# Inverse transform of a spectral mixer: 64-row products in pairs for the odd residues, and folds in two steps

## The chip, the cores and the metric

The kernel runs on one core of a Trainium2 chip. The metric is the device time of one execution in microseconds. The engines are TensorE (PE, with its weight loads as PEld), VectorE (DVE), ScalarE (ACT), GpSimd (POOL) and SyncE (SP); the last issues most transfers. Matmuls write to PSUM, of which the kernel uses eight banks: four called acc, two fa, two fb.

## The reference

Two mixers work on the same shape of input, 2048 rows by 512 columns in bf16, and a gate mixes them row by row:

```
g = sigmoid((x * gate_w).sum(-1, keepdims=True))        # x = A_x
a = irfft2(rfft2(x) * (w_r + 1j * w_i), s=(2048, 512))  # axes: rows, columns; stored as bf16
h = layernorm(B_x)                                      # over the 512 columns
u = gelu(einsum("bsd,sf->bdf", h, w1) + b1)             # s = 2048, f = 1792
b = (einsum("bdf,fs->bds", u, w2) + b2).transpose(0, 2, 1)
out = g * a + (1 - g) * b
```

In this kernel the gate, the filter and the layernorm all read A_x.

## The kernel before

Rows are split as s = 512 q + 4 p + r, with q and r from 0 to 3 and p the partition. A tile of 128 rows is one pair (q, r).

Four lines of work share the engines.

- The token MLP: 224 matmuls of 512 columns for the first layer (L716, into acc, fa and fb), a GELU on ScalarE (L732), and 224 matmuls' worth of 512 columns for the second (L1028), whose results ScalarE evicts with gate and bias (L1034). The last tile is cut into 256, 128 and 128 columns (acc, fa, fb), and VectorE finishes it (L1041).
- The forward transform: radix-4 sums over q on VectorE, matmuls with cosine and sine tables over p (L565 to L568), a second radix-4 step, and the column transform (L664).
- The spectral product with W, all on VectorE (L831 to L853), followed by a radix-4 step of the inverse (L596 to L612).
- The inverse transform, in three stages. The first (lines 885 to 923) multiplies the spectrum, the tile B, with the table ti, for each residue r, each column parity h and two sets of wavenumbers: lt = 0 holds the even ones, lt = 1 the odd ones. Rows p below 64 of lt = 0 carry the wavenumbers 4p, rows from 64 on 2 + 4(p - 64). For even r each product has 128 columns and VectorE folds the results into the tile zz (zf, L931 to L937). For odd r (L903) each product has 256 columns, two accumulate (real and imaginary), and ScalarE casts the bank straight into zz (L918). For lt = 0 and odd r the second 128 table columns repeat the first with the sign turned for rows from 64 on. The second stage (fq, L943 and L944) sums and subtracts over lt and writes the products' sums z. The third (L986 to L990) multiplies z with the table tg; ScalarE evicts with the gate (L994); VectorE then folds each pair of tiles: an edge copy (L1009), two operations into a buffer es (L1010, L1011), two from es back (L1012, L1013), and finally the sum with the MLP's output (L1047). The last pair, called late, also adds the bias (L1007).

The order of the work is decided when the kernel is built. Every piece is a task with an engine, a duration, what it reads and writes, a priority and the buffers it allocates and frees (add, in the class Plan). A list scheduler (Plan.order) walks through time with these durations; on each engine it places the ready task with the lowest priority number whose buffers are free. The tasks are then emitted in that order, and each engine works through its own in it. The second layer's matmuls have high priority numbers (20 and more) and fill whatever PE time the transform (priorities 0 to 4) leaves. The buffers acc, fa, fb, es and the weights wa, wb are counted in caps; NES is the number of es buffers. In the first inverse stage, before the change, a product of lt = 0 takes a bank fa and one of lt = 1 a bank fb.

Of the kernel before, what the change touches and what calls it, by code (L numbers as in the profile page):

```python
# [13 lines left out]
BF16 = mybir.dt.bfloat16  # L14
F32 = mybir.dt.float32

P = 128
# [5 lines left out]
L = 256  # L23
# [7 lines left out]
def ti_at(r):  # L31
    return (0, 1024, 512, 1920)[r], (512, 896)[r % 2]
# [106 lines left out]
class Plan:  # L139
# [11 lines left out]
    def add(self, eng, dur, emit, reads=(), writes=(), prio=0.0, alloc=(), free=(), nbytes=0, after=(), late=0.0):  # L151
        t = Task()
        t.late = late
        t.eng, t.dur, t.emit, t.prio = eng, dur, emit, prio
        t.alloc, t.free, t.nbytes = tuple(alloc), tuple(free), nbytes
        t.users, t.end, t.ready = [], None, 0.0
        deps = set(after)
        for k in reads:
            if k in self.last_w:
                deps.add(self.last_w[k])  # L160
            self.readers.setdefault(k, []).append(t)
        for k in writes:
            if k in self.last_w:
                deps.add(self.last_w[k])
            deps.update(self.readers.get(k, ()))
            self.last_w[k] = t
            self.readers[k] = []
        deps.discard(t)
        t.deps = deps
        self.tasks.append(t)  # L170
        return t
# [73 lines left out]
def tt(n):  # L245
    return 0.07 + n / 1920.0
# [10 lines left out]
def act(n, ptr=0):  # L257
    return 0.065 + 0.09 * ptr + n / 1200.0


def mm(*ns):
    return sum(max(n, 62) / 2400.0 + 0.0025 for n in ns)
# [3 lines left out]
def tiny(k):  # L266
    return 0.09 * k + 0.06
# [3 lines left out]
def kernel(  # L271
# [14 lines left out]
    V, A, T = nc.vector, nc.scalar, nc.tensor  # L286
# [7 lines left out]

    pool = ctx.enter_context(tc.tile_pool(name="sb", bufs=1))
    psum = ctx.enter_context(tc.tile_pool(name="ps", bufs=1, space=bass.MemoryType.PSUM))
    NES = 1

    def sb(shape, dt, tag, bufs=1):
        return pool.tile(shape, dt, tag=tag, name=tag, bufs=bufs)  # L300

    def ps(shape, dt, tag, bufs):
        return psum.tile(shape, dt, tag=tag, name=tag, bufs=bufs)
# [4 lines left out]
    add = pl.add  # L308
    t = {}
# [64 lines left out]
    for r in range(4):  # L374
# [3 lines left out]
        else:  # L378
            for qs in ((0,), (1,), (2, 3)) if r == 1 else ((0, 1, 2, 3),):
                c = slice(qs[0], qs[-1] + 1)  # L380
# [93 lines left out]
    for r in range(4):  # L474
# [3 lines left out]
        for b, qs in enumerate(groups):  # L478
# [8 lines left out]
            for j in js:  # L487
# [14 lines left out]
                if j == 8:  # L502
# [8 lines left out]
                    after=[rect[0, 0]] if j == 4 else ())  # L511
# [23 lines left out]
            for j in js:  # L535
                if j in HACT:
                    add("ACT", 0.71, lambda j=j: A.activation(t["h"][:, j // 4, j % 4, :], t["x"][:, j // 4, j % 4, :], ActF.Identity,  # L537
                                                                  bias=t["nmr"][:, j:j + 1], scale=t["rstd"][:, j:j + 1]),
                        reads=xb + [("rstd", *g)] + mvk, writes=[("h", j)], prio=-0.5 + 0.1 * r)
# [198 lines left out]
    gates = []  # L738
# [136 lines left out]
    for lt in range(2):  # L875
# [5 lines left out]
        if lt == 0:  # L881
            add("SP", 0.5, lambda: dma(t["B"][0:1, 0].rearrange("p e (c v) l -> p (e c) (v l)", c=2), t["s8"][P - 8:P]),
                reads=["s8"], writes=[("T", 0, 0), ("T", 0, 1)], prio=0, nbytes=8192)

    i1t = {}
    for rs, h in ((0, 0), (0, 1), (1, 0), (1, 1)):
        for r in (rs, rs + 2):
            for lt in range(2):
                tag = ("fa", "fb")[lt]

                def i1(h=h, r=r, lt=lt, tag=tag):
                    if "zz" not in t:
                        t["zz"] = sb([P, 2, 2, 2, 2, 2, 2, P], BF16, "X")
                        t["ze"] = sb([P, 2, 2, 2, 2, L], BF16, "h")
                    p1 = t["i1", h, r, lt] = ps([P, 2, L], F32, tag, 2)
                    o, w = ti_at(r)
                    ti = t["ti"][:, o:o + w]
                    for v in range(2):
                        d = lambda c: t["B"][:, lt, r, 2 * c + v, h:L:2]
                        if r % 2:  # L900
                            for c in range(2):
                                f = (2 * c if lt == 0 else 5 - c) * P
                                T.matmul(p1[:, v], lhsT=d(c), rhs=ti[:, f:f + L], start=(c == 0), stop=(c == 1))  # L903
                        else:
                            u = ti[:, 256 * lt:256 * lt + 256]
                            if r == 0 and lt == 0:
                                T.matmul(p1[:, v, 65:256], lhsT=d(1), rhs=t["ti"][:, 2816:3007], start=True, stop=False)
                                T.matmul(p1[:, v, 128:192], lhsT=d(0), rhs=u[:, 66:130], start=False, stop=True)
                                T.matmul(p1[:, v, 0:65], lhsT=d(0), rhs=u[:, 0:65], start=True, stop=True)
                            else:  # L910
                                T.matmul(p1[:, v, P:], lhsT=d(1), rhs=u[:, P:], start=True, stop=True)
                                T.matmul(p1[:, v, 0:P], lhsT=d(0), rhs=u[:, 0:P], start=True, stop=True)
                i1t[h, r, lt] = add("PE", mm(*([256] * 4 if r % 2 else [128] * 4 if r or lt else [191, 64, 65] * 2)), i1, reads=[("T", lt, r % 2), "ti"] + ([("T", lt, 1)] if r == 2 else []), writes=[("i1", h, r, lt)], prio=3, alloc=[tag])

                def i1ev(h=h, r=r, lt=lt):
                    if r % 2:
                        o = t["zz"][:, 1, h, lt, :, :, r // 2, :]
                        A.copy(o, t["i1", h, r, lt][:].rearrange("p v (k a) -> p v k a", k=2))  # L918
                    else:
                        o, i = t["ze"][:, h, r // 2, lt], t["i1", h, r, lt][:]  # L920
                        if r == 0 and lt == 0:
                            o, i = o.rearrange("p v (n w) -> p v n w", w=2), i.rearrange("p v (w n) -> p v n w", w=2)
                        A.copy(o, i)
                add("ACT", act(512), i1ev, reads=[("i1", h, r, lt)] + pbk, writes=[("zz" if r % 2 else "ze", h, r, lt)], prio=1.7, free=[tag], after=[lined])

            if r % 2 == 0:
                def zf(h=h, r=r):
                    e = t["ze"][:, h, r // 2]
                    k0, k1 = (t["zz"][:, 0, h, :, :, k, r // 2, :] for k in range(2))
                    if r == 0:  # L930
                        V.tensor_copy(k0[:, :, :, 0], e[:, :, :, 0])  # L931
                        V.tensor_copy(k1[:, :, :, 0], e[:, :, :, P])
                        V.tensor_add(k0[:, :, :, 1:P], e[:, :, :, 1:P], e[:, :, :, P + 1:L])
                        V.tensor_sub(k1[:, :, :, P - 1:0:-1], e[:, :, :, 1:P], e[:, :, :, P + 1:L])
                    else:
                        V.tensor_add(k0, e[:, :, :, 0:P], e[:, :, :, P:L])
                        V.tensor_sub(k1[:, :, :, ::-1], e[:, :, :, 0:P], e[:, :, :, P:L])  # L937
                add("DVE", 2 * tt(512) + (tiny(2) if r == 0 else 0), zf, reads=[("ze", h, r, lt) for lt in range(2)], writes=[("zz", h, r, lt) for lt in range(2)], prio=3.55)

        def fq(rs=rs, h=h):  # L940
            z = xph(h)[:, 2048 * rs:2048 * rs + 2048].rearrange("p (q v n) -> p q v n", q=4, v=2)
            a, b = (t["zz"][:, rs, h, i].rearrange("p v k r a -> p k v (r a)") for i in range(2))
            V.tensor_add(z[:, 0:4:3], a, b)  # L943
            V.tensor_sub(z[:, 1:3], a[:, ::-1], b[:, ::-1])  # L944
        add("DVE", 2 * tt(1024), fq, reads=[("zz", h, r, lt) for r in (rs, rs + 2) for lt in range(2)] + [("T", 0, 0), ("T", 0, 1), ("T", 1, 0), ("T", 1, 1)],
            writes=[("z", rs, h)] + ([] if rs else ["pp" if h else "xs"]), prio=3.6)
# [27 lines left out]
    for p in range(NJ // 2):  # L974
# [23 lines left out]
        def tb2j(j0=j0):  # L998
            tbuf(j0)
            return t["tb_"][:, j0:j0 + 3:2]  # L1000

        def es(p=p, j0=j0, late=late, tb2j=tb2j):
            e, s = eo_v(p), sb([P, 2, 2, 2, P], BF16, "es", NES)
            o = tb2j() if late else e
            if late:
                for i in range(2):
                    V.tensor_scalar_add(e[:, i, 0, 0:129], e[:, i, 0, 0:129], t["ombb2"][:, j0 + 2 * i:j0 + 2 * i + 1])  # L1007
            o = o.rearrange("p j h (k d) -> p j (h k) d", k=2)
            V.tensor_copy(s[:, :, :, :, 0], e[:, :, :, 0:129:128].rearrange("p j h k -> p j k h"))  # L1009
            V.tensor_add(s[:, :, 0, :, 1:P], e[:, :, :, 1:P], e[:, :, :, P + 1:L])  # L1010
            V.tensor_sub(s[:, :, 1, :, P - 1:0:-1], e[:, :, :, 1:P], e[:, :, :, P + 1:L])  # L1011
            V.tensor_add(o[:, :, 0:4:3], s[:, :, :, 0], s[:, :, :, 1])  # L1012
            V.tensor_sub(o[:, :, 2:0:-1], s[:, :, :, 0], s[:, :, :, 1])  # L1013
        add("DVE", 0.2 + tiny(1) + 4 * tt(512) + (0.3 if late else 0), es, reads=(k1 + ["omg"]) if late else [],
            writes=ko if late else k1, prio=4, alloc=["es"], free=["es"], after=gates if late else ())

        for i, j in enumerate((j0, j1)):
            n = 2 * p + i
# [77 lines left out]
```

## Time and profile before

| | us |
|---|---|
| median of three runs | 126.31 (126.26 to 126.35) |
| the profiled execution | 126.59 |
| its span, first to last instruction | 124.8 |
| TensorE busy | 121.2 (97% of the span) |
| VectorE busy | 113.4 (91%) |
| ScalarE busy | 82.6 (66%) |

The granted TensorE clock was 1.000 over the span. The first inverse stage lies at about 90.4 to 99 us, the third stage and the folds at 99 to 118, and the last store is issued at 122.4. A row of the timeline gives start, length, engine, line, operation and output from input; in a group's row, the count, the busy time, the mean of one in ns and the idle time before it follow. The recorded duration of a matmul includes its way through the array, so neighbouring ones overlap; the distance between two starts is what one costs in a stream. The chain is followed back from the last instruction and says which work set the end.

### The profile page before, as it was taken

What the parts mean: (1) busy time and instruction counts of PE and PEld (TensorE: products, weight loads), DVE (VectorE), ACT (ScalarE), POOL (GpSimd) and SP (SyncE); (2) the same over time, 40 slices, a digit from 0 to 9 for tenths busy, and PEclk for the clock granted to TensorE, in tenths of its full rate; (3) what the DMA queues carried; (4) which work ended last, traced back from release to release, by engine and by line L of the source; (5) the groups of instructions that cost most, each with busy time, mean ns of one, the idle gap of its engine ahead of it and who ended that gap; (6) DMA issues with size and microseconds to landing.
All of it is one profiled execution on the core that took longest, in us unless ns stands there. A gap on an engine that the chain in (4) does not pass through costs nothing.

```text
span 124.8 us, 2188 instructions
## 1 busy us (share of the span) xinstructions
PE 121.2 (97%) x773; PEld 68.8 (55%) x773; DVE 113.4 (91%) x274; ACT 82.6 (66%) x169; POOL 0.2 (0%) x4
## 2 busy tenths in 40 slices
PE   7999999999999999999999999999999999999990
PEld 2345655555655466744455555555578767655590
DVE  1889999999989999999999999999979999999961
ACT  3795889699999999999520003742289999952200
POOL 0000000000000000000000000000000000000000
PEclk9999999999999999999999999999999999999999
DMA  4998999994649936799999900000000000011751
GB/s 122 347 302 277 397 395 389 375 294 86 145 87 302 266 74 156 226 411 414 417 420 415 377 17 0 0 5 0 3 0 0 0 5 0 0 63 45 318 205 47
DMA packets 18202, 23.09 MB, mean 185 GB/s; under 512 B 2174, under 2 KB 15888, under 8 KB 18192
## 3 DMA queue, kind: packets, MB, share of 16 engines
q1 hardware_dynamic: 17616, 22.34, 52.6%
q10 hardware_dynamic: 576, 0.62, 1.6%
q8 instruction: 6, 0.10, 0.3%
q14 instruction: 4, 0.03, 0.1%
HBM read 20.84 MB, written 2.10 MB: 184 GB/s over the span
## 4 chain that ended last, share of the span: by engine, by line
PE 97%; DVE 0%; issue 0%
PE acc L1028 33%; PE acc L716 31%; PE fb L716 6%; PE fb L1028 5%; PE fa L361 4%; PE fa L716 3%; PE fa L664 1%; PE fb L664 1%; PE fa L903 1%; PE fa L566 1%; PE fb L903 1%; PE fa L565 1%; PE fb L990 1%; PE fa L990 1%; PE fa L568 1%; PE fa L567 1%
## 5 line engine op out<-in xcount | busy, mean ns | idle before, releaser
L716 PE MATMUL acc<-h,wb 128*128 128x512 bf16 x112 | 27.0, 379 | 0.0
L1028 PE MATMUL acc<-gl,wb 128*128 128x512 bf16 (+1 forms) x98 | 24.5, 372 | 0.0
L1028 PE MATMUL acc<-gl,wa 128*128 128x512 bf16 (+1 forms) x98 | 23.8, 372 | 0.0
L1034 ACT ACTIVATE x<-acc,ombb,omg 128x512 bf16<-128x512 f32 x12 | 9.1, 782 | 20.8 <-PE acc L1028 20.8
L1028 PEld LDWEIGHTS <-wa 128*128 128x128 bf16 x126 | 13.4, 113 | 9.9
L1028 PEld LDWEIGHTS <-wb 128*128 128x128 bf16 x126 | 13.3, 114 | 9.2
L716 PE MATMUL acc<-h,wa 128*128 128x512 bf16 x64 | 17.4, 385 | 0.0
L716 PEld LDWEIGHTS <-wb 128*128 128x128 bf16 x112 | 10.7, 98 | 10.3
L716 PEld LDWEIGHTS <-wa 128*128 128x128 bf16 x112 | 10.4, 99 | 10.5 <-issue 0.7
L571 ACT CAST xp<-fa 128x512 bf16<-128x512 f32 x16 | 9.1, 584 | 2.4 <-PE fa L568 2.3
L746 ACT ACTIVATE x<-x 128x512 bf16<-128x512 bf16 x16 | 10.0, 649 | 0.0
L716 PE MATMUL fb<-h,wa 128*128 128x512 bf16 x32 | 9.9, 379 | 0.0
L489 DVE BATCH_NORM_STATS2 stats<-x 128x6 f32<-128x512 bf16 x12 | 8.1, 676 | 1.9 <-DMA x<-in_A_x_dram 1.9
L732 ACT ACTIVATE gl<-acc,b1f 128x512 bf16<-128x512 f32 x11 | 7.7, 701 | 2.8 <-PE acc L716 2.8
L537 ACT ACTIVATE h<-x,nmr,rstd 128x512 bf16<-128x512 bf16 x11 | 8.4, 808 | 1.1 <-DVE nmr L528 1.1
L716 PE MATMUL fa<-h,wa 128*128 128x512 bf16 x16 | 6.3, 392 | 0.0
L664 PEld LDWEIGHTS <-X 128*128 128x128 bf16 x64 | 4.7, 98 | 2.2
L994 ACT ACTIVATE B<-fa,g 128x512 bf16<-128x512 f32 x8 | 5.8, 727 | 0.0
L994 ACT ACTIVATE B<-fb,g 128x512 bf16<-128x512 f32 x8 | 5.8, 719 | 0.0
L361 PE MATMUL fa<-const-float32-0.0 128*128 128x512 bf16 x10 | 4.4, 629 | 0.8 <-PEq L1080 0.8
L671 ACT CAST X<-fb 128x512 bf16<-128x512 f32 x8 | 5.1, 638 | 0.0
L671 ACT CAST X<-fa 128x512 bf16<-128x512 f32 x8 | 5.1, 634 | 0.0
(176 smaller groups left out, 235.9 us busy)
## 6 DMA issues: line engine op xcount, KB each, us to landing
wb<-in_B_w_dram SPq DMA_DIRECT2D x11, 512.0 KB
wa<-in_B_w_dram SPq DMA_DIRECT2D x7, 512.0 KB
wa<-in_B_w_dram SPq DMA_DIRECT2D x2, 896.0 KB
wb<-in_B_w_dram SPq DMA_DIRECT2D x4, 384.0 KB
out_dram<-x SPq DMA_DIRECT2D x3, 512.0 KB
x<-in_A_x_dram SPq DMA_DIRECT2D x2, 512.0 KB
wa<-in_B_w_dram SPq DMA_DIRECT2D x4, 224.0 KB
rot<-dft_ti SPq DMA_DIRECT2D x1, 768.0 KB
```

Of the source, the lines that this page charges most:

```text
L361: T.matmul(pw[:], lhsT=zero[:, 0:1].to_broadcast([P, P]), rhs=zero[:, 0:1].to_broadcast([P, D]), start=True, stop=True)
L489: V.bn_stats(out=t["stats"][:, j, :], in_=t["x"][:, j // 4, j % 4, :])
L537: add("ACT", 0.71, lambda j=j: A.activation(t["h"][:, j // 4, j % 4, :], t["x"][:, j // 4, j % 4, :], ActF.Identity, bias=t["nmr"][:, j:j ...
L571: add("ACT", act(512), lambda r=r, dq=dq: A.copy(xe(r)[:, :, :, dq, :], t["pa", r, dq][:]), reads=[("pa", r, dq)], writes=[("X", r, dq)], ...
L664: T.matmul(pb[:, k % 2, k // 2], lhsT=t["X"][:, lt, EX[e], c, k, :], rhs=tbl(k, c), start=True, stop=True)
L671: A.copy(t["X"][:, lt, EX[e]].rearrange("p c j l -> p (c j l)").rearrange("p (h c g b) -> p h c g b", h=2, c=2, b=2)[:, :, c], t["pb", lt, ...
L716: T.matmul(t["u", ft][:], lhsT=w[:, j // 4, j % 4, c * P:(c + 1) * P], rhs=t["h"][:, j // 4, j % 4, :], start=(j == jorder[0]), stop=(j == ...
L732: gelus.append(add("ACT", act(512, 1) , lambda ft=ft: A.activation(t["gl"][:, ft, :], t["u", ft][:], ActF.Gelu_apprx_tanh, bias=t["b1f"][: ...
L746: A.activation(t["x"][:, q, r, :], t["x"][:, q, r, :], ActF.Copy, accum_out=t["glog"][:, 4 * q + r:4 * q + r + 1])
L994: A.activation(eo_v(p)[:, n].rearrange("p h (n w) -> p h n w", w=2), t["i3", j][:].rearrange("p h (w n) -> p h n w", w=2), ActF.Copy, scal ...
L1028: T.matmul(t["y", j, m][:, cs], lhsT=w[:, o, 512 * q + r:512 * q + 512:4], rhs=t["gl"][:, ft, cs], start=(ft == 0), stop=(ft == NFT - 1))
L1034: A.activation(tbuf(j).rearrange("p h d -> p (h d)"), t["y", j, 0][:], ActF.Identity, bias=t["ombb2"][:, j:j + 1], scale=t["omg"][:, j:j + 1])
```

## The change

In the first inverse stage, for odd r and lt = 0, the products with 256 table columns are replaced. For each parity h one task (i1s) now issues sixteen matmuls of 128 columns: for r = 1 and 3, both halves v and both parts c, the same product is made over rows 0 to 63 into a bank fa and over rows 64 to 127 into a bank fb. ScalarE casts both banks into a new area zo (in the tile that also holds ze), and VectorE writes their sum and their difference into zz (eo2), which are the two halves that the 256 columns gave. The products of lt = 1 stay; they now alternate between fa and fb by r. MMR is the duration that the planner assumes for i1s.

In the folds, es has two buffers instead of one; the edge copy goes to ScalarE as a task of its own (ese), except for the last pair; and the fold is two tasks (es and es2) where it was one.

```diff
-    NES = 1
+    NES = 2
...
+    MMR = 8 * mm(128) + 0.1
...
+        if rs:
+            def i1s(h=h):
+                p2 = t["i1s", h] = [ps([P, 2, 2, P], F32, tag, 2) for tag in ("fa", "fb")]
+                for n, r in enumerate((1, 3)):
+                    ti = t["ti"][:, ti_at(r)[0]:]
+                    for v in range(2):
+                        for c in range(2):
+                            for m in range(2):
+                                k = slice(64 * m, 64 * m + 64)
+                                T.matmul(p2[m][:, n, v], lhsT=t["B"][k, 0, r, 2 * c + v, h:L:2], rhs=ti[k, 2 * c * P:2 * c * P + P], start=(c == 0), stop=(c == 1))
+            i1t[h, 1, 0] = i1t[h, 3, 0] = add("PE", MMR, i1s, reads=[("T", 0, 1), "ti"], writes=[("i1s", h)], prio=3, alloc=["fa", "fb"])
+            for m in range(2):
+                add("ACT", act(512), lambda h=h, m=m: A.copy(t["zo"][:, h, m], t["i1s", h][m][:]), reads=[("i1s", h)] + pbk, writes=[("zo", h, m)],
+                    prio=1.7, free=[("fa", "fb")[m]], after=[lined])
+
+            def eo2(h=h):
+                for k, f in enumerate((V.tensor_add, V.tensor_sub)):
+                    f(t["zz"][:, 1, h, 0, :, k].rearrange("p v r a -> p r v a"), t["zo"][:, h, 0], t["zo"][:, h, 1])
+            add("DVE", 2 * tt(512), eo2, reads=[("zo", h, m) for m in range(2)], writes=[("zz", h, r, 0) for r in (1, 3)], prio=3.55)
         for r in (rs, rs + 2):
-            for lt in range(2):
-                tag = ("fa", "fb")[lt]
+            for lt in range(rs, 2):
+                tag = ("fa", "fb")[lt if not rs else r // 2]
...
-                                f = (2 * c if lt == 0 else 5 - c) * P
+                                f = (5 - c) * P
...
+        def edge(f, s, e):
+            f(s[:, :, :, :, 0], e[:, :, :, 0:129:128].rearrange("p j h k -> p j k h"))
+
+        if not late:
+            def ese(p=p):
+                t["es", p] = sb([P, 2, 2, 2, P], BF16, "es", NES)
+                edge(A.copy, t["es", p], eo_v(p))
+            add("ACT", 0.22, ese, reads=[("eo", j0), ("eo", j1)], writes=[("es", p)], prio=1.4, alloc=["es"])
...
-            V.tensor_copy(s[:, :, :, :, 0], e[:, :, :, 0:129:128].rearrange("p j h k -> p j k h"))
+            if late:
+                edge(V.tensor_copy, s, e)
             V.tensor_add(s[:, :, 0, :, 1:P], e[:, :, :, 1:P], e[:, :, :, P + 1:L])
             V.tensor_sub(s[:, :, 1, :, P - 1:0:-1], e[:, :, :, 1:P], e[:, :, :, P + 1:L])
+            t["es", p] = s, o
+
+        def es2(p=p):
+            s, o = t["es", p]
             V.tensor_add(o[:, :, 0:4:3], s[:, :, :, 0], s[:, :, :, 1])
             V.tensor_sub(o[:, :, 2:0:-1], s[:, :, :, 0], s[:, :, :, 1])
...
+        add("DVE", (0.15 if late else 0.02) + 2 * tt(512) + (0.3 if late else 0), es, reads=(k1 + ["omg"]) if late else [("es", p)],
+            writes=[("es", p)] + (ko if late else k1), prio=4, alloc=["es"] if late else [], after=gates if late else ())
+        add("DVE", 2 * tt(512), es2, reads=[("es", p)], writes=ko if late else k1, prio=3.95, free=["es"])
```

More of the change, by code (lines that the diff above doesn't have):

```diff
@@ L893, in i1 @@
                         t["zz"] = sb([P, 2, 2, 2, 2, 2, 2, P], BF16, "X")
-                        t["ze"] = sb([P, 2, 2, 2, 2, L], BF16, "h")
+                        hb = sb([P, 8192], BF16, "h")
+                        t["ze"] = hb[:, 0:4096].rearrange("p (h r i v n) -> p h r i v n", h=2, r=2, i=2, v=2)
+                        t["zo"] = hb[:, 4096:6144].rearrange("p (h m r v n) -> p h m r v n", h=2, m=2, r=2, v=2)
                     p1 = t["i1", h, r, lt] = ps([P, 2, L], F32, tag, 2)
@@ L1000, in tb2j @@
             return t["tb_"][:, j0:j0 + 3:2]
+        def edge(f, s, e):
[5 more added lines that the diff above has]
+            add("ACT", 0.22, ese, reads=[("eo", j0), ("eo", j1)], writes=[("es", p)], prio=1.4, alloc=["es"])
         def es(p=p, j0=j0, late=late, tb2j=tb2j):
-            e, s = eo_v(p), sb([P, 2, 2, 2, P], BF16, "es", NES)
+            e, s = eo_v(p), sb([P, 2, 2, 2, P], BF16, "es", NES) if late else t["es", p]
             o = tb2j() if late else e
@@ L1008, in es @@
             o = o.rearrange("p j h (k d) -> p j (h k) d", k=2)
-            V.tensor_copy(s[:, :, :, :, 0], e[:, :, :, 0:129:128].rearrange("p j h k -> p j k h"))
+            if late:
+                edge(V.tensor_copy, s, e)
             V.tensor_add(s[:, :, 0, :, 1:P], e[:, :, :, 1:P], e[:, :, :, P + 1:L])
             V.tensor_sub(s[:, :, 1, :, P - 1:0:-1], e[:, :, :, 1:P], e[:, :, :, P + 1:L])
+            t["es", p] = s, o
+        def es2(p=p):
+            s, o = t["es", p]
             V.tensor_add(o[:, :, 0:4:3], s[:, :, :, 0], s[:, :, :, 1])
             V.tensor_sub(o[:, :, 2:0:-1], s[:, :, :, 0], s[:, :, :, 1])
-        add("DVE", 0.2 + tiny(1) + 4 * tt(512) + (0.3 if late else 0), es, reads=(k1 + ["omg"]) if late else [],
-            writes=ko if late else k1, prio=4, alloc=["es"], free=["es"], after=gates if late else ())
+        add("DVE", (0.15 if late else 0.02) + 2 * tt(512) + (0.3 if late else 0), es, reads=(k1 + ["omg"]) if late else [("es", p)],
+            writes=[("es", p)] + (ko if late else k1), prio=4, alloc=["es"] if late else [], after=gates if late else ())
+        add("DVE", 2 * tt(512), es2, reads=[("es", p)], writes=ko if late else k1, prio=3.95, free=["es"])
         for i, j in enumerate((j0, j1)):
```

## The prediction

> **What bounds the kernel now.** I read the page's head and its chain first, then the list of waits, then the chain in order of time around the changed stage, then the timelines of VectorE and of the tail.
>
> ```profile
> span 124.8 us, 2188 instructions
> PE 121.2 (97%) x773; PEld 68.8 (55%) x773; DVE 113.4 (91%) x274; ACT 82.6 (66%) x169; POOL 0.2 (0%) x4
> PE   7999999999999999999999999999999999999990
> DVE  1889999999989999999999999999979999999961
> PEclk9999999999999999999999999999999999999999
> ...
> PE 97%; DVE 0%; issue 0%
> ...
> ACT x L1034 <- PE acc L1028: 20.8, 6, 12.3
> PE fa L361 <- PEq L1080: 0.8, 1, 0.8
> ```
>
> TensorE (PE) holds 97% of the chain at full clock. The waits (engine, line, what it waited for; total, times, longest) have one row for PE: 0.8 us before its first instruction. Busy time alone would not prove saturation, since matmul records overlap; that no wait interrupts the chain does. So time taken out of PE's stream should come off the end, unless an engine behind it is late there. The end itself:
>
> ```profile
> 119.08 0.74 DVE L1041 SCALAR_TENSOR_TENSOR x<-acc,omg,x 128x512 bf16<-128x512 f32 x1
> 120.43 0.48 DVE L1041 SCALAR_TENSOR_TENSOR x<-acc,omg,x 128x256 bf16<-128x256 f32 x1 [0.60 <-PE acc L1028]
> 121.21 0.35 DVE L1041 SCALAR_TENSOR_TENSOR x<-fa,omg,x 128x128 bf16<-128x128 f32 x1 [0.29 <-PE fa L1028]
> 121.99 0.35 DVE L1041 SCALAR_TENSOR_TENSOR x<-fb,omg,x 128x128 bf16<-128x128 f32 x1 [0.43 <-PE fb L1028]
> ```
>
> VectorE (DVE) waits 0.60 + 0.29 + 0.43 = 1.32 us for PE here. That is DVE's slack against PE; after it only the last store is left. The profiled execution took 126.59 us, 1.79 of them around the span and 0.28 above the median of 126.31.
>
> **The change, part by part: the products.** The even-wavenumber odd-residue products are the L903 matmuls into fa. The chain in order of time (start, length, what) gives their true price, start to start; the groups give the recorded durations:
>
> ```profile
> 93.99 0.44 PE fa L903 x4
> ...
> 94.87 0.44 PE fb L903 x4
> 95.31 0.44 PE fa L903 x4
> ...
> 108.93 11.46 PE acc L1028 x60
> ...
> 47.09 0.22 PE fa L664 x4
> ...
> L903 PE MATMUL fa<-rot,B 128*128 128x256 bf16 x16 | 2.4, 273 | 0.0
> L912 PE MATMUL fb<-rot,B 128*128 128x128 bf16 x8 | 1.2, 219 | 0.0
> L903 PEld LDWEIGHTS <-B 128*128 128x128 bf16 x32 | 3.1, 98 | 0.8
> ```
>
> Removed: 16 matmuls of 256 columns, four groups of 0.44 (0.436 from neighbouring starts), 1.74 us of PE. Added: two groups of 16 matmuls of 128 columns over 64 rows each, alternating lower rows into fa and upper rows into fb. A 128-column matmul with its own weight load takes 0.22/4 = 55 ns. If the two halves of a pair run side by side, a group is 8 x 55 = 0.44 us, two are 0.89, and the gain is 0.85. If they run one after the other, it is 32 x 55 = 1.76: no gain.
>
> No run before has a 64-row matmul, so the overlap is bounded by these two ends, 0.85 and -0.02 us. I take overlap: the halves use different array rows, different input rows and different banks, and nothing in the stream shows PE short of instructions. Each pair also wants two weight loads in its 55 ns. The nearest rows are two consecutive 64-column matmuls:
>
> ```profile
> 99.06 0.25 PE L986 MATMUL fa<-tg,xp 128*128 128x191 bf16 x1
> 99.14 0.19 PE L987 MATMUL fa<-tg,xp 128*128 128x64 bf16 x1
> 99.17 0.20 PE L988 MATMUL fa<-tg,xp 128*128 128x65 bf16 x1
> ...
> 99.14 0.10 PEld L988 LDWEIGHTS <-xp 128*128 128x128 bf16 x1
> ...
> 91.97 0.22 PE L911 MATMUL fb<-rot,B 128*128 128x128 bf16 x1
> ...
> 92.02 0.10 PEld L911 LDWEIGHTS <-B 128*128 128x128 bf16 x1
> ```
>
> The second matmul starts 0.03 us after its own load started, so a load need not cost its recorded 98 ns. Two at 30 ns are 60 per pair instead of 55: 16 pairs x 0.005 = 0.07 us lost.
>
> The second unknown is the passage from 128-row to 64-row matmuls and back: four times in all. The nearest rows are changes of table, width and tile, which cost nothing (L987 follows L986 after 0.08, its 191 columns at the rate of the others). The other end: the next matmul starts only when the last has left the array. A 128-column matmul is recorded with 219 ns and spaced by 55, so 164 ns would stay uncovered, 4 x 0.164 = 0.66 us; with the next load also held back, 98 ns more each, 1.05. The changes without cost are nearer in kind than a complete stop, but none changes the rows, so I take half of the 164: 4 x 0.082 = 0.33.
>
> The Trainium skill, TensorEngine Tiling (Array Packing), Key Properties, says that changing the tiling mode drains TensorE; it gives no duration. By it the full 0.66 would be due and the gain would be 0.13 us. No row of this trace can say whether it does so; it is the first rival.
>
> **PE's sum:** 0.85 - 0.07 - 0.33 = 0.45 us off. Waits: one task now needs a free bank in fa and in fb at once, and what queues behind it on PE are the L1028 matmuls and so everything to the end. The planner only places it where both are free, with L1028 as filler. Nothing of PE before 90 us is touched.
>
> **Sum and difference on VectorE.** Four tensor operations of 128x512 are added. The same form, by neighbouring starts in the timeline, is spaced by 0.33:
>
> ```profile
> 94.95 0.42 DVE L936 TENSOR_TENSOR X<-h 128x512 bf16<-128x512 bf16 x1
> 95.29 0.42 DVE L937 TENSOR_TENSOR X<-h 128x512 bf16<-128x512 bf16 x1
> ...
> 102.39 0.42 DVE L1013 TENSOR_TENSOR B<-es 128x512 bf16<-128x512 bf16 x1
> 102.91 0.19 DVE L1009 COPY es<-B 128x8 bf16<-128x8 bf16 x1
> 103.00 0.42 DVE L1010 TENSOR_TENSOR es<-B 128x508 bf16<-128x508 bf16 x1
> 103.33 0.42 DVE L1011 TENSOR_TENSOR es<-B 128x508 bf16<-128x508 bf16 x1
> 103.86 0.42 DVE L1012 TENSOR_TENSOR B<-es 128x512 bf16<-128x512 bf16 x1
> ```
>
> That is 4 x 0.335 = +1.34 us, on an engine that is dense from 93 us until 119.8. They stand before the products z, so the third stage's matmuls on PE (L986 to L990) start up to 1.3 us later; L1028 work covers that, of which 11.46 us in one piece still follow the last L990 now (the row from 108.93). ScalarE's number of casts stays (eight for the odd residues).
>
> **The folds.** Seven edge copies leave DVE: 0.08 from start to start (102.91 to 103.00), -0.58. Splitting and double-buffering can close holes: L1011 to L1012 is 0.53 against 0.33 for independent operations, 0.19 lost, and L1013 to L1009, 0.52, loses 0.18. At 0.19 for seven pairs and 0.18 at the three places where a copy follows a fold directly, at most 1.9. DVE's balance is thus +1.34 - 0.58 = +0.76 if no hole closes, and -1.1 if all do; I take the middle, -0.2, since two pairs must be ready at once. Even +0.76, together with 0.45 less on PE, is 1.21 against the slack of 1.32. So I cost it at nothing; the cover is the three waits at the tail, and beyond 0.87 of extra DVE work each further microsecond is a microsecond at the end.
>
> The copies go to ScalarE (ACT). The nearest rows:
>
> ```profile
> L780 ACT CAST W<-fa 128x8 bf16<-128x8 f32 x1 | 0.3, 276 | 0.0
> L748 ACT ACTIVATE g<-glog 128x16 f32<-128x16 f32 x1 | 0.2, 215 | 0.0
> ...
> 110.51 0.68 ACT L994 ACTIVATE B<-fb,g 128x512 bf16<-128x512 f32 x1
> ...
> 116.47 0.42 DVE L1007 TENSOR_SCALAR B<-B,ombb 128x129 bf16<-128x129 bf16 x2
> ```
>
> Seven by 0.22 to 0.28 is +1.5 to 1.9 us. ACT's last third-stage eviction (110.51 + 0.68 = 111.19) would end at about 113, and DVE takes up the last pair at 116.47, so 3 us of cover remain. New wait: a copy needs its fold buffer back from DVE two pairs earlier; behind it on ACT stand evictions, which free the banks of PE. The 20.8 us that ACT waits for acc (first fence) show that these banks have time.
>
> No DMA or its queue is moved; the last store keeps its place. So the sum is -0.45 us: 126.59 becomes 126.14 for the profiled execution, 125.86 for the median.
>
> **Rivals.** First, every passage between row modes stops PE. With 0.66 the gain is 0.13 (126.18, no change); with the weight load held back too, 0.85 - 0.07 - 1.05 = -0.27 (126.58). For it: 164 ns really are in flight at any moment. Against: nothing before stops. It turns the sign from 195 ns per passage.
>
> Second, the ending on the other side that I take most seriously: the pairs don't overlap, so the change does not do what it says. 32 x 55 ns instead of 1.74 us is +0.02, with the four passages at 0.33 it is 126.66; with 0.66, 126.99. For it: no matmul here has ever started before the previous one's columns were through. It decides from 87 ns a pair (1.74 - 0.33 over 16 pairs).
>
> Third, a weight load may not overlap a matmul in flight on the same rows. Then each pair pays 98 ns on top of 55: 16 x 0.153 = 2.45 against 1.74, plus the passages 0.33: 127.35. Against it: the load at 92.02 runs while the matmul that started at 91.97, on all 128 rows, is in flight until 92.19. The Trainium skill, TensorE: Matmul & The Clock Gate, Part 3, What overlaps and what doesn't, says that loads overlap matmuls in flight only where the row group differs. By it the third rival would hold; these two rows disagree with it.
>
> Fourth, PE waits for the second bank. One ACT cast is spaced by 0.48 (next fence), and twice that is +0.96: 126.82. It needs ACT to run behind its plan there, and no wait for a bank exists now.
>
> ```profile
> 95.38 0.68 ACT L918 CAST X<-fa 128x512 bf16<-128x512 f32 x1
> 95.86 0.69 ACT L918 CAST X<-fb 128x512 bf16<-128x512 f32 x1
> ```
>
> Fifth, DVE or ACT becomes late at the end: the folds' new dependence on ACT opens holes instead of closing them. Seven new holes of 0.18 on +0.76 make +2.0 of DVE, 0.7 beyond the slack of 1.32, so 126.31 + 0.70 = 127.0.
>
> **How the numbers follow.** Forecast 0.55 (its own range 125.46, with passages and loads free, to 126.05, where 0.2% lies); first rival 0.18, half at each of its times; second 0.13; third 0.03; fourth 0.06; fifth 0.05. A change of 0.2%, 0.25 us, is about what a measurement of this kernel can tell from none. Faster: the forecast and a sliver of the first rival, 0.57. Same: the milder half of the first rival with the edges of the second, 0.13. Slower: the rest, 0.30. The range goes from 125.4 to 126.75, which leaves out about 2 in 10: most of the third to fifth rivals and the dearer end of the second.
>
> **What would show it.** Right: 64-row matmuls whose starts come in pairs within 30 ns, a group over in 0.45 to 0.5 us; a hole of 50 to 100 ns at its edges; no PE wait in the list; the last fb matmul about 0.45 us earlier; DVE still waiting for PE in the three L1041 rows. Starts evenly 55 ns apart would show the second rival, holes of 160 ns or more the first, a PE wait for ACT the fourth, a DVE with no wait in the last L1041 row the fifth. The prediction is wrong if PE's stream shortens but the tail does not follow, or if the order of the filler matmuls opens waits that no row of before shows.

## The result and the profile after

The changed kernel takes 126.09 us (median), the one before 126.43 in the runs beside it: a ratio of 0.9973, 95% interval 0.9964 to 0.9982, or 0.34 us less. The profiled executions are 126.11 and 126.59 us; of these 0.48 us, 0.10 lie ahead of the change, since the first product of the stage starts at 90.32 instead of 90.42.

The head of the page, its chain, and two rows of the list of waits (engine, line, what it waited for; total, times, longest), all of the changed kernel:

```profile
span 124.3 us, 2226 instructions
PE 119.8 (96%) x789; PEld 67.7 (54%) x789; DVE 113.2 (91%) x271; ACT 83.7 (67%) x176; POOL 0.2 (0%) x4
...
PE 93%; DMA 2%; DVE 1%; ACT 0%; issue 0%
...
ACT x L1071 <- PE acc L1065: 19.3, 6, 12.3
PE fa L716 <- DVE h L531: 0.9, 1, 0.9
```

TensorE still sets the end. Its one new wait, 0.9 us for a normalised tile in the first layer, stands at the very start of the program, where the order of instructions is the same in both kernels; it is no effect of the change. L1065 and L1071 are the former L1028 and L1034.

The second of the two new groups in the timeline (start, length, engine, line, operation, output from input, count):

```profile
97.22 0.62 PE L1065 MATMUL acc<-gl,wb 128*128 128x512 bf16 x2
97.77 0.23 PE L897 MATMUL fa<-rot,B 64*128 64x128 bf16 x1
97.78 0.23 PE L897 MATMUL fb<-rot,B 64*128 64x128 bf16 x1
97.84 0.22 PE L897 MATMUL fa<-rot,B 64*128 64x128 bf16 x1
97.84 0.22 PE L897 MATMUL fb<-rot,B 64*128 64x128 bf16 x1
...
98.17 0.22 PE L897 MATMUL fa<-rot,B 64*128 64x128 bf16 x1
98.18 0.22 PE L897 MATMUL fb<-rot,B 64*128 64x128 bf16 x1
98.33 0.41 PE L1065 MATMUL acc<-gl,wb 128*128 128x512 bf16 x1
...
97.77 0.45 PEld L897 LDWEIGHTS <-B 64*128 64x128 bf16 x16 [0.41 <-issue]
```

The halves of a pair start within 10 ns of each other, and pairs follow each other after 55 ns. The second filler matmul starts at 97.22 + 0.62 - 0.38 = 97.46 and streams for 0.22, to 97.68; the group starts 0.09 later. The last pair is through at 98.23, and the next filler starts 0.10 later. The first pair is followed 11 ns later than the others, and that filler is stretched by 28 ns (407 instead of 379). So from filler to filler a group costs 0.68 us, 0.45 of it products and 0.23 the two passages between row modes. Before, the same products cost 2 x 0.436 = 0.87. The gain is 0.19 per parity, 0.39 in all, which agrees with the 0.38 of the profiled executions behind the start offset and with the 0.34 of the medians. The PEld row shows that the weight loads do not fill the hole: the sixteen begin with the group, where loads otherwise run ahead during the matmul before. What holds both back is not shown.

VectorE's folds now alternate between two pairs, and the tail keeps all its waits:

```profile
102.62 0.42 DVE L1042 TENSOR_TENSOR es<-B 128x508 bf16<-128x508 bf16 x1
102.95 0.42 DVE L1043 TENSOR_TENSOR es<-B 128x508 bf16<-128x508 bf16 x1
103.29 0.42 DVE L1042 TENSOR_TENSOR es<-B 128x508 bf16<-128x508 bf16 x1
103.62 0.42 DVE L1043 TENSOR_TENSOR es<-B 128x508 bf16<-128x508 bf16 x1
103.96 0.42 DVE L1048 TENSOR_TENSOR B<-es 128x512 bf16<-128x512 bf16 x1
...
117.49 0.68 DVE L1084 TENSOR_TENSOR x<-x,B 128x1024 bf16<-128x1024 bf16 x1
118.41 0.75 DVE L1078 SCALAR_TENSOR_TENSOR x<-acc,omg,x 128x512 bf16<-128x512 f32 x1 [0.23 <-PE acc L1065]
119.94 0.48 DVE L1078 SCALAR_TENSOR_TENSOR x<-acc,omg,x 128x256 bf16<-128x256 f32 x1 [0.78 <-PE acc L1065]
120.72 0.35 DVE L1078 SCALAR_TENSOR_TENSOR x<-fa,omg,x 128x128 bf16<-128x128 f32 x1 [0.30 <-PE fa L1065]
121.50 0.35 DVE L1078 SCALAR_TENSOR_TENSOR x<-fb,omg,x 128x128 bf16<-128x128 f32 x1 [0.43 <-PE fb L1065]
121.89 0.35 ACTq L312 DMA_DIRECT2D out_dram<-x  x1
```

In the kernel before:

```profile
118.48 0.68 DVE L1047 TENSOR_TENSOR x<-x,B 128x1024 bf16<-128x1024 bf16 x1
122.37 0.35 ACTq L312 DMA_DIRECT2D out_dram<-x  x1
```

Every 0.33 us one operation starts, with no hole between dependent halves. The last sum (L1084, formerly L1047) starts at 117.49, where the kernel before had it at 118.48: VectorE is 0.99 us earlier although four operations were added. Of this 0.10 is the earlier start of the stage, so the change itself is worth 0.89. From the last issue of a store, 121.89, to the end of the span are 2.4 us, as before (122.37 to 124.8).

### The profile page after: what moved, and what is told of

It reads as the page before. It is cut to its first block, busy times and chain, and to the rows that moved or that the text cites. A ratio compares the mean times of both kernels' runs of the same rounds, so it can differ in the third digit from the quotient of the medians.

```text
span 124.3 us, 2226 instructions
## 1 busy us (share of the span) xinstructions
PE 119.8 (96%) x789; PEld 67.7 (54%) x789; DVE 113.2 (91%) x271; ACT 83.7 (67%) x176; POOL 0.2 (0%) x4
## 4 chain that ended last, share of the span: by engine, by line
PE 93%; DMA 2%; DVE 1%; ACT 0%; issue 0%
PE acc L1065 33%; PE acc L716 31%; PE fb L716 6%; PE fb L1065 6%; PE fa L716 3%; DMA x<-in_A_x_dram 2%; PE fb L664 1%; PE fa L664 1%; PE fa L565 1%; PE fa L566 1%; PE fa L897 1%; PE fb L1012 1%; PE fa L1012 1%; PE fa L568 1%; PE fa L567 1%; PE fb L925 1%
## 5 line engine op out<-in xcount | busy, mean ns | idle before, releaser
L1065 PE MATMUL acc<-gl,wb 128*128 128x512 bf16 (+1 forms) x98 | 24.7, 372 | 0.0
L1065 PE MATMUL acc<-gl,wa 128*128 128x512 bf16 (+1 forms) x98 | 24.0, 371 | 0.0
L1071 ACT ACTIVATE x<-acc,ombb,omg 128x512 bf16<-128x512 f32 x12 | 9.0, 780 | 19.3 <-PE acc L1065 19.3
L1065 PEld LDWEIGHTS <-wa 128*128 128x128 bf16 x126 | 13.4, 113 | 9.6
L1065 PEld LDWEIGHTS <-wb 128*128 128x128 bf16 x126 | 13.2, 114 | 9.4
L741 DVE TENSOR_TENSOR x<-x,gw 128x2048 bf16<-128x2048 bf16 x4 | 4.7, 1214 | 0.0
```

The source lines that it names most:

```text
L741: add("DVE", tt(2048), lambda r=r: V.tensor_mul(t["x"][:, :, r, :], t["x"][:, :, r, :], t["gw"][:, None, :].to_broadcast([P, 4, D])), read ...
L1065: T.matmul(t["y", j, m][:, cs], lhsT=w[:, o, 512 * q + r:512 * q + 512:4], rhs=t["gl"][:, ft, cs], start=(ft == 0), stop=(ft == NFT - 1))
L1071: A.activation(tbuf(j).rearrange("p h d -> p (h d)"), t["y", j, 0][:], ActF.Identity, bias=t["ombb2"][:, j:j + 1], scale=t["omg"][:, j:j + 1])
```

## The experiments

The questions are two: is it the overlap of the row halves, less the passages, that sets TensorE's gain, and what part do the folds play? Each time is given against the median of the kernel before in the runs beside it. The profiled executions reach the inverse stage at slightly different moments, 90.13 to 90.46 us in the runs whose spans are compared here; where that matters, times are counted from the first product of the stage.

**The passages: none, two, many.** The first run leaves out the split by rows: eight products over all 128 rows go into one bank, which ScalarE casts twice, so the sum and the difference no longer come from two halves.

```diff
-                            for m in range(2):
-                                k = slice(64 * m, 64 * m + 64)
-                                T.matmul(p2[m][:, n, v], lhsT=t["B"][k, ...], rhs=ti[k, ...], ...)
...
+                            T.matmul(p2[0][:, n, v], lhsT=t["B"][:, ...], rhs=ti[:, ...], ...)
...
```

> Leaves out the split by rows: eight products of 128 columns over all 128 rows per parity, into one bank that ScalarE casts twice; casts, sum and difference stay. Columns in PE's stream are as many as the pairs take, but there is no passage between row modes. If the passages cost 0.225 us per group, this is 0.45 us under the changed kernel: 125.65 us. If the pairs themselves are what costs (halves not quite side by side) and passages are free, the products still start 55 ns apart and the gain over the changed kernel shows inside the group, not at its edges.

125.61 us against 126.53, ratio 0.9936 (0.9914 to 0.9959): by the ratios 0.37%, or 0.47 us, below the changed kernel, where 0.45 was expected and the two passages of each group add up to 0.46. In its timeline the eight products follow the filler without a hole (the second filler starts at 96.08 + 0.59 - 0.38 = 96.29, the group 0.22 later) and what follows starts 0.45 later:

```profile
96.08 0.59 PE L1063 MATMUL acc<-gl,wb 128*128 128x512 bf16 x2
96.51 0.61 PE L895 MATMUL fa<-rot,B 128*128 128x128 bf16 x8
96.96 0.60 PE L923 MATMUL fa<-rot,B 128*128 128x256 bf16 x4
```

So a pair of halves costs no more than one full product; all that the split costs lies at its edges. The second run makes one group of the two parities, in one task with four banks (the planner's test for free banks counts them accordingly):

```diff
-            i1t[h, 1, 0] = i1t[h, 3, 0] = add("PE", MMR, i1s, ..., writes=[("i1s", h)], prio=3, alloc=["fa", "fb"])
...
+                one = add("PE", 2 * MMR - 0.1, both, ..., writes=[("i1s", 0), ("i1s", 1)], prio=3, alloc=["fa", "fb", "fa", "fb"])
```

> The changed kernel with the products of both parities in one task of four banks, so two passages between row modes instead of four. By the passage theory (about 0.095 us to enter, 0.10 to leave and 0.025 on the next matmul) it gains 0.2 us on the changed kernel: 125.9 us, about 0.6 us under the kernel before. The rival, a wait of PE for four free banks, expects a PE wait of up to 1 us in the list and 126.3 us or more.

125.87 us against 126.53, ratio 0.9948 (0.9933 to 0.9963): 0.25% below the changed kernel's ratio, and no wait for a bank in its list. Four free banks at once were to be had without cost. This version beats both kernels.

```diff
                     for v in range(2):
+                        if n or v:
+                            T.matmul(p2[0][:, n, v], lhsT=t["B"][:, 0, 1, v, h:L:2], rhs=t["ti"][:, 0:P], start=True, stop=True)
                         for c in range(2):
```

> The changed kernel with one extra 128-row matmul of 128 columns between each two of the four accumulated product sets of a parity (three per parity, six in all; their results are overwritten by the products that follow). The six extra matmuls cost 6 x 0.056 = 0.33 us by themselves. If every passage into and out of 64-row mode costs what the trace of the changed kernel shows (0.10 + 0.12 us), twelve more passages add 6 x 0.22 = 1.32: 127.75 us. If only the change from the long filler matmuls to the group costs something, the time is 126.4 us.

127.59 us against 126.42, ratio 1.0107 (1.0016 to 1.0198): by the ratios 1.69 us above the changed kernel, where 1.66 was expected. The interval is wide, though it leaves out the other expectation (126.4), and the timeline shows the same price again, from one pair to the next across the inserted matmul:

```profile
96.53 0.22 PE L899 MATMUL fa<-rot,B 64*128 64x128 bf16 x1
96.53 0.22 PE L899 MATMUL fb<-rot,B 64*128 64x128 bf16 x1
96.68 0.23 PE L895 MATMUL fa<-rot,B 128*128 128x128 bf16 x1
96.84 0.23 PE L899 MATMUL fa<-rot,B 64*128 64x128 bf16 x1
96.84 0.23 PE L899 MATMUL fb<-rot,B 64*128 64x128 bf16 x1
```

0.31 us from 96.53 to 96.84, of which 0.11 are the columns of a pair and of the inserted matmul: 0.20 for two passages, also between short matmuls. The Trainium skill, TensorEngine Tiling (Array Packing), Key Properties, says that changing the tiling mode drains TensorE; a hole at every change agrees with that. The holes are 0.09 to 0.10 us each, shorter than the 0.164 that the prediction took for a complete way through the array, so whether the array is empty at a change is not shown.

**Side by side, or just smaller.**

```diff
-                for n, r in enumerate((1, 3)):
...
-                    for v in range(2):
-                        for c in range(2):
-                            for m in range(2):
...
+                for m in range(2):
...
+                    for n, r in enumerate((1, 3)):
...
+                        for v in range(2):
+                            for c in range(2):
...
```

> The changed kernel with the same sixteen matmuls per parity in another order: eight over the lower rows, then eight over the upper rows. If the gain rests on the two halves running side by side, neighbours now share their rows and start 55 ns apart: 16 x 55.6 ns more over both parities, 0.89 us, 126.98 us. If TensorE is simply quicker with 64-row products, or finds the overlap by itself, the time stays at 126.1 us.

126.47 us against 126.42, ratio 0.9990 (0.9957 to 1.0023). The interval holds both the kernel before and the changed kernel, so the profile has to decide. Counted from the start of the stage (90.25), its span is 0.48 us longer than the changed kernel's and 0.09 longer than the one before the change (34.49 against 34.01 and 34.40 us): the gain is gone, but only about half of the expected loss came. The timeline of its first group:

```profile
96.60 0.45 PE L897 MATMUL fa<-rot,B 64*128 64x128 bf16 x5
96.84 0.23 PE L897 MATMUL fb<-rot,B 64*128 64x128 bf16 x1
96.89 0.22 PE L897 MATMUL fa<-rot,B 64*128 64x128 bf16 x1
96.91 0.22 PE L897 MATMUL fb<-rot,B 64*128 64x128 bf16 x1
96.94 0.22 PE L897 MATMUL fa<-rot,B 64*128 64x128 bf16 x1
96.96 0.22 PE L897 MATMUL fb<-rot,B 64*128 64x128 bf16 x1
97.00 0.22 PE L897 MATMUL fa<-rot,B 64*128 64x128 bf16 x1
97.02 0.44 PE L897 MATMUL fb<-rot,B 64*128 64x128 bf16 x5
97.39 0.41 PE L1065 MATMUL acc<-gl,wb 128*128 128x512 bf16 x1
```

Matmuls on the same half follow each other after 55 to 60 ns, as expected. But the first upper one (fb), ninth in the program, starts at 96.84, ahead of the sixth, seventh and eighth (96.89 to 97.00); the second group shows the same. From there the halves run side by side, so a group grows by 0.24 us and not by 0.45. Both theories of the expectation were wrong in the pure form: the gain needs the overlap, and TensorE finds part of it by itself.

**The folds.** One run has the new folds with the old products, one the new products with the old folds. The first, against the kernel before:

```diff
-    NES = 1
+    NES = 2
...
+            add("ACT", 0.22, ese, ...)
...
+        add("DVE", 2 * tt(512), es2, ...)
```

> The new folds with the products of before. VectorE gets about 2.4 us more room at the end (edge copies on ScalarE, holes closed), PE's stream is unchanged: by the theory that PE alone bounds, the time is that of the kernel before, 126.4 us, ratio 1.000. The rival, that part of the gain comes from VectorE's folds, expects up to 0.2 us less.

126.64 us against 126.53, ratio 1.0003 (0.9988 to 1.0018): no difference. Alone the folds lengthen VectorE's waits for TensorE (2.3 us for acc in its list).

The second, against the changed kernel:

```diff
-    NES = 2
+    NES = 1
...
-            add("ACT", 0.22, ese, ...)
...
-        add("DVE", 2 * tt(512), es2, ...)
```

> The 64-row pairs with the folds of the kernel before (one es buffer, edge copy on VectorE, one task). PE's stream is that of the changed kernel, about 0.40 us shorter than before. By the slack theory VectorE carries the four extra operations, 1.34 us, with nothing taken off; with PE 0.40 us earlier that is 1.74 against the slack of 1.32 us, so the end comes about 0.4 us later than in the changed kernel: 126.5 us, no faster than before, and VectorE no longer waits for PE ahead of its first L1041-type operation. The rival, that the folds play no part and PE alone sets the end, expects the changed kernel's 126.1 us.

127.37 us against 126.53, ratio 1.0072 (1.0053 to 1.0091): with the old folds the new products make the kernel slower. TensorE's stream is as short as in the changed kernel, but VectorE no longer waits anywhere in the tail:

```profile
119.93 0.69 DVE L1069 TENSOR_TENSOR x<-x,B 128x1024 bf16<-128x1024 bf16 x1
120.53 1.14 DVE L1063 SCALAR_TENSOR_TENSOR x<-acc,omg,x 128x512 bf16<-128x512 f32 x2
121.58 0.34 DVE L1063 SCALAR_TENSOR_TENSOR x<-fa,omg,x 128x128 bf16<-128x128 f32 x1
121.84 0.34 DVE L1063 SCALAR_TENSOR_TENSOR x<-fb,omg,x 128x128 bf16<-128x128 f32 x1
122.22 0.35 ACTq L312 DMA_DIRECT2D out_dram<-x  x1
```

The direction was expected, the size not: 126.5 was forecast. VectorE ends at 122.18, earlier than before the change (122.34), and yet the span ends at 125.5. Two milder doses bracket the point from which it costs. The first has es and es2 in one task again; two buffers and the edge copy on ScalarE stay:

```diff
-            t["es", p] = s, o
-
-        def es2(p=p):
-            s, o = t["es", p]
...
```

> The changed kernel with two fold buffers and the edge copies on ScalarE, but each fold in one task, so the dependent halves follow each other directly. VectorE loses about 0.19 us per pair again, 1.3 us in all, and ends about 0.2 us later than in the kernel before. By the slack theory this still hides behind PE: 126.1 us. If the interleaving of two pairs is what carries the change, 126.6 us or more.

126.22 us against 126.42, ratio 0.9972 (0.9946 to 0.9997): as the changed kernel. Its last sum starts at 118.97, 0.49 us later than in the kernel before; the stage starts 0.29 earlier (90.13), so VectorE carries 0.78 us more there. One wait is left in the list for the tail:

```profile
118.97 0.68 DVE L1079 TENSOR_TENSOR x<-x,B 128x1024 bf16<-128x1024 bf16 x1
119.57 1.14 DVE L1073 SCALAR_TENSOR_TENSOR x<-acc,omg,x 128x512 bf16<-128x512 f32 x2
120.63 0.34 DVE L1073 SCALAR_TENSOR_TENSOR x<-fa,omg,x 128x128 bf16<-128x128 f32 x1
121.31 0.35 DVE L1073 SCALAR_TENSOR_TENSOR x<-fb,omg,x 128x128 bf16<-128x128 f32 x1 [0.34 <-PE fb L1060]
```

The other is the run with the products alone, with two buffers:

```diff
-    NES = 1
+    NES = 2
```

> The products with the old one-task fold and VectorE's edge copies, but two fold buffers: of the changed folds only the hole at three pairs goes, 0.54 us. VectorE then has about 0.9 us more than before the change and reaches the end just as TensorE does. By the slack of 1.32 us with TensorE 0.40 us earlier, 126.2 us; if the bunching of the last stores counts as soon as VectorE no longer waits for TensorE, between 126.4 and 127.0 us.

126.85 us against 126.58, ratio 1.0024 (1.0006 to 1.0041). The last sum starts at 119.54; counted from the stage (90.46) that is 1.01 us later than in the kernel before. The list has no wait in the tail any more, but the chain in order of time still comes from TensorE:

```profile
120.83 0.80 PE fb L1050 x14
121.62 0.03 issue
121.65 0.35 DVE x L1063
```

The last operation starts at 121.65, only 0.15 us after the changed kernel's, and 0.14 of that is the later start of the stage; yet the span is 0.8 us longer (125.1). So VectorE's last operation is not late at all here, and the loss of about 0.63 us lies behind it, in the stores.

**Where the rest of that delay comes from.** In the late runs the end comes 3.0 to 3.2 us after the last store is issued instead of 2.4 (122.38 from SyncE to 125.5 with the products alone). The semaphore events in the traces split this distance: a store has landed when its semaphore has its last increment, and the closing instructions of the program follow (times in us).

| run | stage starts | last four stores issued within | last issue | last landing, after the issue | end, after the landing |
|---|---|---|---|---|---|
| before | 90.42 | 2.52 | 122.37 | 1.49 | 0.95 |
| changed kernel | 90.32 | 2.70 | 121.89 | 1.49 | 0.95 |
| folds in one task | 90.13 | 1.35 | 121.70 | 1.67 | 0.96 |
| products, two buffers | 90.46 | 1.12 | 122.03 | 1.94 | 1.14 |
| products alone | 90.27 | 1.08 | 122.38 | 1.96 | 1.21 |
| products, early sum | 90.16 | 0.91 | 122.52 | 1.85 | 1.20 |
| early sum, one store | 90.46 | two stores | 122.79 | 1.74 | 1.07 |

With the products alone, the 1.21 us that the span is longer than the changed kernel's are about 0.33 at VectorE's last operation, 0.16 more at the issue of the last store, 0.47 in its landing and 0.25 in the closing instructions. Three runs tried to find the reason. The first is the run with the products alone, in which the last fold (es) must now wait for the sum fin2 of the pair before:

```diff
-            add("DVE", tt(1024), fin2, reads=k1, writes=ko, prio=4)
+            fin2t.append(add("DVE", tt(1024), fin2, reads=k1, writes=ko, prio=3.5))
...
```

> As the run with the products alone (old folds), but the last pair's fold must come after the sum that completes the pair before it, so that the 512 KB store which needs that sum leaves about 2 us earlier; VectorE has the same work. If that run was late because the bulk stores bunch up behind the last one, the end moves to the last L1041-type operation plus the usual 2.45 us: about 126.6 us instead of 127.4. If VectorE's load alone made it late, it stays at 127.4 us or rises.

127.63 us against 126.42, ratio 1.0080 (1.0053 to 1.0107). The bulk store did leave earlier, at 118.73 instead of 120.64, and nothing was gained, though it had landed at 121.33, before the next store was issued; that the bulk store stands before the last ones is not the cause.

The second is the changed kernel with the last stores to be held back:

```diff
-                ... + ([("of", j0, m)] if j0 in JS[-2:] else []), prio=50,
+                ... + ([("of", j0, m), ("of", LAST, 2)] if j0 in JS[-2:] else []), prio=50,
```

> The changed kernel with the last four stores (128, 64, 32 and 32 KB) all held back until the very last VectorE operation; TensorE and VectorE have the work of the changed kernel. In the run with the products alone these four were issued within 0.9 us and the end came 3.1 us after the last issue instead of 2.4. If the bunching is what made those runs late beyond VectorE's own delay, the last issue here is at about 122.55 us of the span and the end 3.1 us later: 127.4 us. If only VectorE's load did, the end follows 2.4 us after the last issue: 126.75 us.

126.19 us against 126.58, ratio 0.9966 (0.9952 to 0.9980), but the run says nothing: the edit changes what the planner orders by, the waits follow the data, and the stores left one by one as before.

The third is the run with the early sum, with one store for the last tile after all of its parts:

```diff
-    (15, 16, 1, parts)]
+    (15, 16, 1, [slice(0, D)])]
...
```

> As the run with the products alone and the early sum, but the last tile's three stores of 64, 32 and 32 KB are one store of 128 KB after the very last VectorE operation, from ScalarE's queue. VectorE's work and order are the same. If three small stores, issued one behind the other within 0.9 us, are what adds 0.7 us to the usual 2.4 between the last issue and the end, one store brings the end back to about 2.4 to 2.6 us after it: 126.7 to 126.9 us. If the lateness is VectorE's alone, or lies in the transfer of the last 256 KB whatever its cut, the time stays at 127.6 us or rises.

127.15 us against 126.53, ratio 1.0044 (1.0024 to 1.0064), by the ratios 0.36% or 0.45 us below the run with three small stores, with intervals that overlap. The last issue is at 122.79 and the end 2.8 us later, between the two expectations; in the profiles the distance is 0.23 us shorter than with three stores. So small stores that follow each other closely are probably part of the price, some 0.2 to 0.45 us. Why they land later, and why the closing instructions then take longer, stays open.

## Why the prediction was right or wrong

**Faster, and by how much.** Right. Forecast were 0.45 us off and 125.86; measured are 0.34 us and 126.09, inside the range and on the forecast side. The signs named for it came too: pairs within 10 ns, a group over in 0.46 us, holes of 0.09 to 0.10 us, and three waits in the tail.

**The products.** The step "the two halves of a pair run side by side" is shown, by starts within 10 ns and by the run with full rows, whose group takes as long and differs at its edges. The 0.07 us for two loads per pair was wrong: pairs keep 55 ns.

**The passages.** Half of 164 ns was taken for want of a nearer row, 4 x 0.082 = 0.33. Measured are 0.09 to 0.10 us of hole and 0.01 to 0.03 of stretch each, 0.46 us in all. This is the term that was mis-sized, and with the loads' 0.07 returned TensorE's sum is 0.85 - 0.46 = 0.39 where 0.45 was forecast. That the sum came so near is in part luck: no row of the kernel before bore on the half of 164 ns, and the two errors partly cancel. The first rival, with the drain at 0.164 or more, is out, and so are the second and third; the fourth (a wait for the second bank) did not occur, even with four banks at once. The fifth did not occur: the copies on ScalarE opened no holes in the folds, and a VectorE that is late at the end came only without the new folds.

**VectorE.** The balance was put at -0.2 us and came to -0.89, counted from the start of the stage: that "two pairs must be ready at once" was no obstacle, and nearly all holes closed. The claim that even +0.76 us would cost nothing is not refuted and only roughly shown: at +0.78 (folds in one task) the ratio is that of the changed kernel, but known to about 0.3 us, and the last store already landed 0.18 us later after its issue. The step that failed is the rule "beyond 0.87 us each further microsecond is a microsecond at the end", which counts the last store as a fixed distance behind the last operation. With TensorE's measured 0.39 the limit is 1.32 - 0.39 = 0.93. At +1.01 (two buffers) the rule gives a loss of 0.08 us on the changed kernel; VectorE's last operation lost nothing, and the run lost 0.64 by the ratios. At +1.60 (the products alone) it gives 0.67; the last operation lost 0.39, and the run lost 1.25. For VectorE's operations the slack was thus read well enough; the stores behind them had less. The forecast did not depend on this, since the changed kernel kept its waits.

**ScalarE.** Right: seven copies of 0.21 to 0.24 us are on it, and its waits for acc are 19.3 us where they were 20.8.

## What to carry to other kernels

When one engine's stream is unbroken, taking columns out of it pays even at the cost of work on other engines, but the relief must be bought with their slack: here the products without the new folds made the kernel slower. Products of 64 rows in pairs halve the columns; alternate the halves, and put as many pairs as possible into one group, since each group pays about 0.23 us for entering and leaving. Read slack at the tail to the last store's landing and not to the last computation: here, stores that were issued closely behind each other landed later.

## What the runs showed of the hardware

- Entering a group of 64-row matmuls and leaving it each leave a hole of 0.09 to 0.10 us, beside 512-column and 128-column neighbours alike, and the group's weight loads do not start before the group does.
- Matmuls on different row halves can start out of program order: with eight lower ones issued first, the ninth matmul, on the upper rows, started before the sixth, in both groups. The Trainium skill, TensorE: Matmul & The Clock Gate, Part 3, What overlaps and what doesn't, calls matmuls monotone in start and end; the starts at 96.84 and 96.89 differ from that, and the length of the group agrees with the starts.
- The last store, of 32 KB, landed 1.49 us after its issue where the store before it was issued 0.79 us earlier (before, changed kernel), 1.67 where it was 0.28 (folds in one task), and 1.85 to 1.96 where it was under 0.2 (the three late runs with small stores). The span then ended 0.95 us after the landing in the first two cases and 1.14 to 1.21 in the late ones.
